# Ten of span 0's twelve attention pairs alone, the last two beside the first three products of L1, and weight blocks stored in one run

## The chip, the cores and the metric

The kernel runs on one core of a Trainium2 chip. The metric is the device time of one launch in microseconds, the median of several runs; one further execution was recorded by the profiler. PE is TensorE, DVE is VectorE, ACT is ScalarE, POOL is GpSimd, and SP is the engine whose queue issues most DMAs.

## The reference

An attention with normalised queries and keys is followed by a two-layer feed-forward network. There are 8 batches, 12 heads, 448 positions and a head size of 64; the network is 768 to 2048 to 768. All is float32 in the reference, and the weights come as 64-bit floats.

```python
def rmsnorm(x, g):
    rms = np.sqrt(np.mean(x * x, axis=-1, keepdims=True) + 1e-06)
    return x / rms * g
q_n, k_n = (rmsnorm(q, g_q), rmsnorm(k, g_k))
scores = scale * np.matmul(q_n, k_n.transpose(0, 1, 3, 2))
attn = np.exp(scores - np.max(scores, axis=-1, keepdims=True))
attn = attn / (np.sum(attn, axis=-1, keepdims=True) + 1e-09)
attn_out = np.matmul(attn, v)
...
x = attn_out.transpose(0, 2, 1, 3).reshape(B * S, H * D)
h = x @ w_in
r = np.maximum(h, 0.0)
return (r * r) @ w_out
```

## The kernel before

Two batches make a span, so there are four spans of 896 tokens. A *pair* is two heads of one batch; a span has twelve pairs. A pair's output is one 128-row part of xT, the network's input with the channels on partitions: `xT[:, b, hp]` for batch b of the span and pair hp of the batch.

The two layers are computed with a seven-product scheme (Winograd's form of Strassen's) on 2x2 blocks: the two batches are the two column blocks, and channels are halved on both sides. `A11, S2, S1, S3, A12, A22, S4` name the seven combinations of weight blocks, and T1 to T4 with B11, B21, B22 those of the input. T1 to T4 are made by `combine_x` in xC and in part of xT as pairs come out. For the first layer (L1) there are HF = 8 column blocks f, each with seven products; a product is three matmuls over 448 columns, which the trace shows as six, into one PSUM bank. Its results are added up by DVE (z, y, and the sums g22, g21, g12) and squared after a relu. The product of A22 accumulates in the bank pd on top of S3, and S4 in pc on top of S1, after DVE has read the first one. A product takes a *block* of weights, `sw`, which SP loads from DRAM (`w1s`, `w2s`) five products ahead (`load_blocks`). The second layer (L2) does the same with gT and gC.

There are two forms of attention. Pairs with i < NAT (the twelve of span 0) are done *alone* by `attention_alone`: keys in four chunks of 112, sums by a matmul with ones (`total_of`), transposes by PE, the square root on ACT and DVE (`roots`). The others are done in the *later* form by `attention`, whose steps are interleaved with L2's products of the span before: four 64x64 matmuls side by side on PE, sums by DVE's `add_up` and `fold`, then sent out and spread again by two DMAs that POOL issues (`sums["out"]`, `spread`), a norm with a power on POOL (`norm_by_squares`), transposes by DVE. Then `finish` scales the values with the sums.

The weights are turned from 64-bit floats into float32 and into the seven combinations during span 0, in small steps called ticks: `prepare(t)` has four ticks for each of 32 pieces of weights (t is the piece that enters). A piece takes a load of 768 KB, two activations on ACT (L589, L606), three operations on DVE (L603, L608, L613), the add of the low words (L575 on POOL for the first pieces, L579 on DVE for the others), and on average two sums on POOL (L583). Every second piece ends in a store of 1344 KB by SP. `weights(upto)` runs the ticks up to a number; `EARLY` (52) is the number done in the alone stage and `ALL` (140) the end.

The schedule is written by hand: each engine executes its instructions in the order of the Python code, which the generators' `yield` interleave. Blocks that have not been stored can't be loaded, so the ticks come ahead of the products that need them.

Of the kernel before, what the change touches and what calls it, by code (L numbers as in the profile page):

```python
# [10 lines left out]
F32 = mybir.dt.float32  # L11
# [376 lines left out]
def attention_then_ffn_bounded(  # L388
# [53 lines left out]

    NAT = 2 * NPAIR

# [43 lines left out]

    EARLY, ALL = 4 * 13, 4 * (2 * NFC + 3)
    assert DM == NW and BLOCKS * 8 * HW + EXPS * NW + 2 * NW <= 3 * HF * S and 2 * NW <= 4 * S and HF % 4 == 0  # L490
# [4 lines left out]
    A21 = 7  # L495
    w1s = dram.tile([HF, 7, P, HW], F32, name="w1s")
    w2s = dram.tile([7, HF // 4, P, 4, HW], F32, name="w2s")

# [52 lines left out]
    def prepare(t):  # L551
# [10 lines left out]
        def value(n, half):  # L562
            if not there(n):
                return

            to = ((A11, A12), (A21, A22)) if n < NFC else ((A11, A21), (A12, A22))
            places = [place_of(n, k) for k in to[n % 2]]
            part = slice(half * HW, (half + 1) * HW)
            if not doubles:
                nc.gpsimd.tensor_copy(blocks_of(n)[:, places[half]], words_of(n).bitcast(F32)[:, part])  # L570
                return
            _, eu, low, _ = parts(n)
            if n < EARLY // 4:
                dst = blocks_of(n)[:, places[half]]
                nc.gpsimd.tensor_tensor(*[x.bitcast(I32) for x in (dst, low[:, part], eu[:, part])], ALU.add)  # L575
            elif half == 0:
                dst = blocks_of(n)[:, places[0]:places[1] + 1:places[1] - places[0]]
                low, eu = (x.rearrange("p (h m) -> p h m", h=2) for x in (low, eu))
                nc.vector.tensor_tensor(*[x.bitcast(I32) for x in (dst, low, eu)], ALU.add)  # L579
# [14 lines left out]
        if there(n) and n % 2:  # L594
            c = n % NFC // 2
            dst = w1s[c] if n < NFC else w2s[:, c // 4, :, c % 4]
            first = place_of(n, A11)
            nc.sync.dma_start(dst.rearrange("k p m -> p k m"), blocks_of(n)[:, first:first + 7])
            written[0] = n + 1
# [43 lines left out]
    uses2 += [(m, i) for m in range(HC) for i in (S2, S1, S3, A22, S4)]  # L643
    def order_of(span, f):

        return (A11, A12, S2, S1, S3, A22, S4) if span == f == 0 else range(7)

# [3 lines left out]
    def load_blocks(upto):  # L651

        while len(stream) < min(upto, NSPAN * (N1 + N2)):
            n = len(stream) % (N1 + N2)
            if written[0] < min(2 * (n // 7 + 1) if n < N1 else 2 * NFC, 2 * NFC):
                return
            sw = loads.tile([P, 4, P], F32, tag="sw", name="sw", bufs=5)
            if n < N1:
                sw = sw[:, 0:HC]
                src = w1s[n // 7, order_of(len(stream) // (N1 + N2), n // 7)[n % 7]].rearrange("p (c m) -> p c m", c=HC)  # L660
            else:
                n -= N1
                m, i = uses2[n // (HF // 4)]
                src = w2s[i, n % (HF // 4), :, :, m * P:(m + 1) * P]
            nc.sync.dma_start(sw, src)
            stream.append(sw)
# [250 lines left out]
    def attention_alone():  # L917


        for i in range(NAT):  # L920
# [22 lines left out]
            if i + 2 < NAT:  # L943
                norm(i + 2)
            elif not more:
                norm(NAT)
                load(NAT + 2)
# [3 lines left out]
            load_v(i + 1)  # L951
            if i + 2 < NAT:
                roots(i + 2)
            yield
            scores(i, 2)
            scores(i, 3)
            total_of(i - 1)
            values(i, (0, 1))
# [5 lines left out]
            if NAT <= i + 3 < NAT + 2:  # L964
                load(i + 3)
            yield
        values(i, (2, 3))
        total_of(i)
        finish(i)
        combine_x(i)  # L970

    def attention(first):


        last = first + 2 * NPAIR
        for i in range(first, last + 1):
# [56 lines left out]

    def first_product(work, span):

# [3 lines left out]
        def activate(g, src):  # L1039
# [3 lines left out]
            else:  # L1043
                nc.gpsimd.tensor_tensor(g, g, g, ALU.mult)  # L1044

        for f in range(HF):
            n = span * (N1 + N2) + f * 7
            order = order_of(span, f)
            g11, g12 = gT[:, f, 0:S], gT[:, f, S:2 * S]
# [3 lines left out]
            for at, i in enumerate(order):  # L1053
# [4 lines left out]
                if first and into == "pa":  # L1058
                    if span == 0 and f:
                        ps_of[into] = ps_o.tile([P, S], F32, tag="ot"[f % 2], name="pa")  # L1060
                    else:
                        ps_of[into] = ps_s.tile([P, 2, 512], F32, tag="s", name="pa")[:, 0, 0:S]
                elif first:
                    ps_of[into] = bank(into)
# [5 lines left out]
                if i == A11:  # L1070
                    p1 = work.tile([P, S], F32, tag="p1", name="p1", bufs=1)
                    nc.scalar.copy(p1, ps)  # L1072
                elif i == S2:
                    z = work.tile([P, S], F32, tag="z", name="z")
                    add(z, p1, ps, ALU.add)  # L1075
                elif i == S1:
                    y = work.tile([P, S], F32, tag="y", name="y")
                    add(y, z, ps, ALU.add)
                elif i == A12:
                    activate(g11, ps)  # L1080
                else:
                    g, x = {S3: (g22, y), A22: (g21, z), S4: (g12, z)}[i]
                    add(g, x, ps, ALU.add)  # L1083
                    activate(g, g)
# [91 lines left out]
    with tc.tile_pool(name="words", bufs=2) as spare["pool"]:  # L1176
# [5 lines left out]
        with tc.tile_pool(name="first", bufs=2, reuse_waits="tile") as work:  # L1182
# [9 lines left out]
            for u, _ in enumerate(attention_alone()):  # L1192

                weights(min(EARLY, 4 + (EARLY - 4) * u // (4 * NAT - 7)))
                if u == 4 * NAT - 9:
                    load_blocks(5)
        with tc.tile_pool(name="first_product", bufs=2, reuse_waits="tile") as work:
            for u, _ in enumerate(first_product(work, 0)):
                if u == 6:

                    left = ps_s.tile([P, 2, 512], F32, tag="s", name="bits")
                    banks["bits"] = left.rearrange("p a b -> p (a b)")[:, 0:NW].bitcast(U32)
                weights(min(ALL, EARLY + (ALL - EARLY) * (u - 1) // (N1 - 6)))
                if u == N1 - 5:
                    norm(NAT + 1)
                if u == N1 - 4:
                    transposes(NAT)
                    squares(NAT + 2)
    for span in range(NSPAN):
# [7 lines left out]
        with tc.tile_pool(name="second_product", bufs=2, reuse_waits="tile") as work:  # L1217
            rest = second_product(work, span)
            if more:
# [4 lines left out]
                total, done, most = HC * (7 * HF + 4) - 20, 0, 10 * NPAIR + 1  # L1224
                for u, _ in enumerate(attention(nxt)):
                    while done < total * min(u + 1, most) // most + 3 * max(u + 1 - most, 0):
                        next(rest)
                        done += 1
# [90 lines left out]
```

## Time and profile before

| | us |
|---|---|
| median of 3 runs (lowest, highest) | 1363.51 (1362.49, 1364.83) |
| the profiled execution's own time | 1362.31 |
| its span | 1360.5 |
| start of the alone stage's second pair to the end of pair 9 | 15.5 to 111.6 |
| pairs 10 and 11 alone | 111.6 to 133.9 |
| L1 of span 0 | 133.9 to 264.9 |
| from L2 of span 0 to the end | 264.9 to 1360.5 |

The span is what the profiler saw from the first to the last instruction; the launch's time has 1.8 us more. A line such as `L1083` is the line of the kernel's file that issued the instruction. "Idle before" is time in which an engine had nothing to do ahead of an instruction, with the instruction or DMA that ended it. A matmul's length overlaps with its neighbours', so PE's rate is read from the distance of starts.

### The profile page before, as it was taken

To read this page: it belongs to the slowest core of one execution; us is meant where nothing else is said; L and a number is where in the kernel's file an instruction comes from. 1 tells how busy PE (TensorE), PEld (TensorE's weight loads), DVE (VectorE), ACT (ScalarE), POOL (GpSimd) and SP (SyncE) were. 2 spreads that over 40 slices of the span, in tenths; PEclk is the share of its full clock that TensorE was granted. 3 is DMA by queue.
4 is the path that set the end of the run, shared out by engine and by line. 5 is a ranking of instruction groups with operands and counts; after the bars stand their busy time and mean duration, and the time that the engine had idled before them with its cause. 6 is when DMAs were issued, how large, how long until landed. Compare 5 with 4: busy or idle time off the path is not lost.

```text
span 1360.5 us, 16880 instructions
## 1 busy us (share of the span) xinstructions
PE 1340.5 (99%) x5618; PEld 641.6 (47%) x5618; DVE 832.1 (61%) x1482; ACT 430.0 (32%) x674; POOL 566.0 (42%) x458
## 2 busy tenths in 40 slices
PE   8999999999999999999999999999999999999998
PEld 3333445444444455444444455444444455555554
DVE  6999788599987333467778523557788633332111
ACT  7886466433332011233332111233333211110000
POOL 5667533466563122655565222446566312220000
PEclk9999999999999999999999999999999999999999
DMA  9777999655685333355675433345765443334443
GB/s 240 208 229 198 314 360 327 183 130 111 130 151 129 99 87 88 100 119 118 135 150 115 113 100 87 101 104 118 142 129 110 105 103 87 87 91 107 106 111 71
DMA packets 434084, 190.12 MB, mean 140 GB/s; under 512 B 282948, under 2 KB 430788, under 8 KB 433988
## 3 DMA queue, kind: packets, MB, share of 16 engines
q1 hardware_dynamic: 427364, 180.33, 52.2%
q0 software_dynamic: 4736, 8.40, 2.5%
q8 instruction: 47, 0.77, 0.2%
q10 hardware_dynamic: 1888, 0.23, 0.1%
q14 instruction: 49, 0.40, 0.1%
HBM read 155.72 MB, written 33.16 MB: 139 GB/s over the span
## 4 chain that ended last, share of the span: by engine, by line
PE 90%; DVE 5%; ACT 3%; DMA 1%; issue 1%; SPq 0%; POOL 0%; ACTq 0%; DVEq 0%
PE ps L1134 37%; PE pd L1068 10%; PE pa L1068 10%; PE pc L1068 10%; PE sc L785 7%; PE pav L862 7%; PE pb L1068 5%; ACT gT L797 1%; DVE gT L810 1%; DVE rstd L715 1%; PE sc L793 1%; DVE gC L613 1%; PE tot L876 1%; DMA gT<-in_moe_w_in_dram 1%; PE pav L851 1%
## 5 line engine op out<-in xcount | busy, mean ns | idle before, releaser
L1134 PE MATMUL ps<-gT,sw 128*128 128x448 f32 x752 | 293.0, 543 | 0.0
L1134 PE MATMUL ps<-gC,sw 128*128 128x448 f32 x576 | 225.2, 543 | 0.0
L1044 POOL TENSOR_TENSOR gT<-gT 128x448 f32<-128x448 f32 x96 | 93.9, 980 | 283.3 <-ACT gT L1040 283.3
L1134 PEld LDWEIGHTS ps<-gT,sw 128*128 128x128 f32 x752 | 141.1, 190 | 146.4 <-issue 142.0
L750 POOL TENSOR_TENSOR half<-half,mhalf 128x28 f32<-128x28 f32 x36 | 175.2, 4868 | 72.7 <-DVE half L749 69.2
L1134 PEld LDWEIGHTS ps<-gC,sw 128*128 128x128 f32 x576 | 108.1, 190 | 112.9 <-issue 110.7
L1068 PE MATMUL pa<-xT,sw 128*128 128x448 f32 x384 | 155.0, 540 | 0.6 <-ACT p L1072 0.6
L1040 ACT ACTIVATE gT<-gT 128x448 f32<-128x448 f32 x96 | 55.3, 577 | 311.2 <-DVE gT L1083 311.2
L787 ACT ACTIVATE pr<-sc 128x896 f32<-128x896 f32 x87 | 77.5, 915 | 121.7 <-PE sc L785 121.7
L785 PE MATMUL sc<-qkT 64*64 64x448 f32 (+1 forms) x1152 | 109.8, 496 | 0.0
L1068 PEld LDWEIGHTS pa<-xT,sw 128*128 128x128 f32 x384 | 72.9, 190 | 72.6 <-issue 70.7
L583 POOL TENSOR_TENSOR gC<-gC 128x384 f32<-128x384 f32 x64 | 76.2, 1209 | 62.2 <-DVE gC L579 60.4
L1083 DVE TENSOR_TENSOR gT<-z,pd 128x448 f32<-128x448 f32 x32 | 19.8, 620 | 97.8 <-PE pd L1068 97.6
L1068 PE MATMUL pd<-xT,sw 128*128 128x448 f32 x192 | 77.9, 542 | 1.3 <-DVE z L1075 1.3
L1068 PE MATMUL pd<-xC,sw 128*128 128x448 f32 x192 | 77.5, 540 | 1.3 <-DVE gT L1083 1.3
L1068 PE MATMUL pb<-xC,sw 128*128 128x448 f32 x192 | 77.5, 540 | 0.1
L752 POOL TENSOR_TENSOR qk<-qk,half 128x448 f32<-128x448 f32 x72 | 76.4, 1081 | 2.8
L1068 PE MATMUL pc<-xC,sw 128*128 128x448 f32 x192 | 77.4, 539 | 0.0
L1068 PE MATMUL pc<-xT,sw 128*128 128x448 f32 x192 | 77.4, 539 | 0.0
L830 POOL DMA_DIRECT2D xT<-factors x72 | 38.0, 532 | 94.7 <-DMA factors<-square 63.9
L862 PE MATMUL pav<-pr,vt 64*64 64x448 f32 x348 | 72.7, 537 | 0.0
L862 PE MATMUL rest<-pr,vt 64*64 64x448 f32 x348 | 72.7, 537 | 0.0
(144 smaller groups left out, 1849.6 us busy)
## 6 DMA issues: line engine op xcount, KB each, us to landing
sw<-w1s SPq DMA_DIRECT2D x224, 192.0 KB, 2.4
sw<-w2s SPq DMA_DIRECT2D x168, 256.0 KB, 3.2
w1s<-gC SPq DMA_DIRECT2D x8, 1344.0 KB, 6.4
w2s<-gC SPq DMA_DIRECT2D x8, 1344.0 KB, 6.1
out_dram<-osb SPq DMA_DIRECT2D x186, 56.0 KB, 1.9
qk<-in_q_dram SPq DMA_DIRECT2D x144, 56.0 KB, 3.5
qk<-in_k_dram SPq DMA_DIRECT2D x144, 56.0 KB, 3.0
xT<-factors POOLq DMA_DIRECT2D x72, 112.0 KB, 3.4
```

The lines of the kernel that those rows point to most:

```text
L583: nc.gpsimd.tensor_tensor(*[blocks_of(n)[:, place_of(n, i)] for i in (dst, x, y)], op)
L750: nc.gpsimd.tensor_tensor(half, half, mhalf, ALU.pow)
L752: nc.gpsimd.tensor_tensor(qkn[:, s], raw[:, s], half[:, s * NG:(s + 1) * NG].rearrange("p g -> p g ()").to_broadcast([P, NG, 32]), ALU.mult)
L785: nc.tensor.matmul(sc[part, h, 0:n], qkT[rows, 0, 1, keys], qkT[rows, 0, 0, of], start=True, stop=True)
L787: nc.scalar.activation(pr, sc[:, :, 0:n], AF.Exp)
L830: nc.gpsimd.dma_start(xT[h * D:(h + 1) * D, b % 2, hp], sums["out"][i % 2].rearrange("(h g) t -> h () (g t)", h=2)[h].to_broadcast([D, S]))
L862: nc.tensor.matmul(into, vs[i][rows, h, c, :], probs[i, c][rows, h, :], start=(c == 0), stop=(c == NF), skip_group_check=True)
L1040: nc.scalar.activation(g, src, AF.Relu)
L1044: nc.gpsimd.tensor_tensor(g, g, g, ALU.mult)
L1068: nc.tensor.matmul(ps, stream[n + at][:, c], rhs[:, c], start=first and c == 0, stop=c == HC - 1, skip_group_check=not first)
L1083: add(g, x, ps, ALU.add)
L1134: nc.tensor.matmul(ps, stream[n][:, c % 4], rhs_of[i][:, c], start=c == 0, stop=c == HF - 1)
```

## The change

NAT becomes ten: pairs 10 and 11 of span 0 are done in the later form. Beside them L1 begins: `first_product(work, 0, 0)` does the three products A11, S1 and A12 of six of the eight column blocks (NE = 6), which need no result of those two pairs. A11's and S1's results are kept in gT by a copy on ACT; A12 accumulates on A11 and is squared. When both pairs are through, the second call does S2, S3, A22 and S4 of those six blocks, and all seven of the last two. For the kept blocks DVE makes y from z and the kept S1, one operation with both inputs in SBUF, and S4 has a bank of its own.

The ticks are spread anew: 48 by the end of the alone stage, 86 by the end of the two pairs, 140 before the end of L1. POOL keeps the add of the low words for 21 pieces instead of 13. `roots` stands behind the last two scores of a pair. Blocks of all seven combinations lie side by side in `w1s` and `w2s`, so a store writes 10,752 bytes in one run per partition instead of seven runs of 1536.

```diff
@@ -440,7 +440,8 @@
     sides = [slice(m * P // 2, (m + 1) * P // 2) for m in range(2)]
-    NAT = 2 * NPAIR
+    NAT = 2 * NPAIR - 2
+    NE = HF - 2
     def start_of(span):
         return 2 * span * NPAIR
@@ -486,15 +487,15 @@
     HW = HC * P
     WORDS, BLOCKS, EXPS = 7, 2, 4
-    EARLY, ALL = 4 * 13, 4 * (2 * NFC + 3)
+    EARLY, MID, ALL = 48, 86, 4 * (2 * NFC + 3)
     assert DM == NW and BLOCKS * 8 * HW + EXPS * NW + 2 * NW <= 3 * HF * S and 2 * NW <= 4 * S and HF % 4 == 0
     A11, S2, S1, S3, A12, A22, S4 = range(7)
     A21 = 7
-    w1s = dram.tile([HF, 7, P, HW], F32, name="w1s")
-    w2s = dram.tile([7, HF // 4, P, 4, HW], F32, name="w2s")
+    w1s = dram.tile([HF, P, 7, HW], F32, name="w1s")
+    w2s = dram.tile([HF // 4, P, 4, 7, HW], F32, name="w2s")
     def pairs_of(words):
         both = words.rearrange("p (n two) -> p n two", two=2)
@@ -570,7 +571,7 @@
                 nc.gpsimd.tensor_copy(blocks_of(n)[:, places[half]], words_of(n).bitcast(F32)[:, part])
                 return
             _, eu, low, _ = parts(n)
-            if n < EARLY // 4:
+            if n < MID // 4:
                 dst = blocks_of(n)[:, places[half]]
                 nc.gpsimd.tensor_tensor(*[x.bitcast(I32) for x in (dst, low[:, part], eu[:, part])], ALU.add)
             elif half == 0:
@@ -593,9 +594,9 @@
         n = t - 3
         if there(n) and n % 2:
             c = n % NFC // 2
-            dst = w1s[c] if n < NFC else w2s[:, c // 4, :, c % 4]
+            dst = w1s[c] if n < NFC else w2s[c // 4, :, c % 4]
             first = place_of(n, A11)
-            nc.sync.dma_start(dst.rearrange("k p m -> p k m"), blocks_of(n)[:, first:first + 7])
+            nc.sync.dma_start(dst, blocks_of(n)[:, first:first + 7])
             written[0] = n + 1
         if there(t) and doubles:
             e, eu, low, high = parts(t)
@@ -641,9 +642,9 @@
     uses2 = [(m, i) for m in range(HC) for i in (A11, A12)]
     uses2 += [(m, i) for m in range(HC) for i in (S2, S1, S3, A22, S4)]
-    def order_of(span, f):
-        return (A11, A12, S2, S1, S3, A22, S4) if span == f == 0 else range(7)
+    first_uses = [(f, i) for f in range(NE) for i in (A11, S1, A12)]
+    first_uses += [(f, i) for f in range(NE) for i in (S2, S3, A22, S4)]
+    first_uses += [(f, i) for f in range(NE, HF) for i in range(7)]
     N1 = HF * 7
     N2 = HC * 7 * (HF // 4)
@@ -651,17 +652,19 @@
     def load_blocks(upto):
         while len(stream) < min(upto, NSPAN * (N1 + N2)):
-            n = len(stream) % (N1 + N2)
-            if written[0] < min(2 * (n // 7 + 1) if n < N1 else 2 * NFC, 2 * NFC):
+            span, n = divmod(len(stream), N1 + N2)
+            if n < N1:
+                f, i = divmod(n, 7) if span else first_uses[n]
+            if written[0] < (2 * (f + 1) if n < N1 and span == 0 else 2 * NFC):
                 return
             sw = loads.tile([P, 4, P], F32, tag="sw", name="sw", bufs=5)
             if n < N1:
                 sw = sw[:, 0:HC]
-                src = w1s[n // 7, order_of(len(stream) // (N1 + N2), n // 7)[n % 7]].rearrange("p (c m) -> p c m", c=HC)
+                src = w1s[f, :, i].rearrange("p (c m) -> p c m", c=HC)
             else:
                 n -= N1
                 m, i = uses2[n // (HF // 4)]
-                src = w2s[i, n % (HF // 4), :, :, m * P:(m + 1) * P]
+                src = w2s[n % (HF // 4), :, :, i, m * P:(m + 1) * P]
             nc.sync.dma_start(sw, src)
             stream.append(sw)
@@ -943,17 +946,16 @@
             if i + 2 < NAT:
                 norm(i + 2)
             elif not more:
-                norm(NAT)
                 load(NAT + 2)
             yield
             if more:
                 transpose(i + 1, 0, 0)
             load_v(i + 1)
-            if i + 2 < NAT:
-                roots(i + 2)
             yield
             scores(i, 2)
             scores(i, 3)
+            if i + 2 < NAT:
+                roots(i + 2)
             total_of(i - 1)
             values(i, (0, 1))
             finish(i - 1)
@@ -963,16 +965,20 @@
             combine_x(i - 1)
             if NAT <= i + 3 < NAT + 2:
                 load(i + 3)
+            if i + 2 >= NAT:
+                norm(i + 2)
             yield
+        transposes(NAT)
         values(i, (2, 3))
         total_of(i)
         finish(i)
         combine_x(i)
-    def attention(first):
-        last = first + 2 * NPAIR
+        if NAT + 2 < 2 * NPAIR:
+            squares(NAT + 2)
+    def attention(first, last):
         for i in range(first, last + 1):
             if i < last:
                 scores(i, 0)
@@ -1031,7 +1037,7 @@
             sub(gC[:, 2, f], g21, gC[:, 1, f], ALU.subtract)
             sub(g12, g22, g12, ALU.subtract)
-    def first_product(work, span):
+    def first_product(work, span, part=1):
         B11, B21, B22 = xT[:, 0, 0:HC], xT[:, 0, HC:], xT[:, 1, HC:]
         T1, T2, T4, T3 = xC[:, 0], xC[:, 1], xC[:, 2], xT[:, 1, 0:HC]
@@ -1043,9 +1049,29 @@
             else:
                 nc.gpsimd.tensor_tensor(g, g, g, ALU.mult)
+        if part == 0:
+            for f in range(NE):
+                turn[0] += 1
+                pa, pc = bank("pa"), bank("pc")
+                for at, (ps, rhs) in enumerate(((pa, B11), (pc, T1), (pa, B21))):
+                    n = 3 * f + at
+                    load_blocks(n + 5)
+                    for c in range(HC):
+                        nc.tensor.matmul(ps, stream[n][:, c], rhs[:, c], start=at < 2 and c == 0,
+                                         stop=c == HC - 1, skip_group_check=at == 2)
+                    if at < 2:
+                        nc.scalar.copy(gT[:, HF + f, at * S:(at + 1) * S], ps)
+                    else:
+                        activate(gT[:, f, 0:S], ps)
+                    yield
+            return
         for f in range(HF):
+            kept = span == 0 and f < NE
+            order = (S2, S3, A22, S4) if kept else range(7)
             n = span * (N1 + N2) + f * 7
-            order = order_of(span, f)
+            if span == 0:
+                n = 3 * NE + 4 * f if kept else 7 * f
             g11, g12 = gT[:, f, 0:S], gT[:, f, S:2 * S]
             g21, g22 = gT[:, HF + f, 0:S], gT[:, HF + f, S:2 * S]
             add = nc.vector.tensor_tensor
@@ -1056,7 +1082,7 @@
                              A12: ("pa", B21), A22: ("pd", T4), S4: ("pc", B22)}[i]
                 first = into not in ps_of
                 if first and into == "pa":
-                    if span == 0 and f:
+                    if span == 0:
                         ps_of[into] = ps_o.tile([P, S], F32, tag="ot"[f % 2], name="pa")
                     else:
                         ps_of[into] = ps_s.tile([P, 2, 512], F32, tag="s", name="pa")[:, 0, 0:S]
@@ -1072,14 +1098,17 @@
                     nc.scalar.copy(p1, ps)
                 elif i == S2:
                     z = work.tile([P, S], F32, tag="z", name="z")
-                    add(z, p1, ps, ALU.add)
+                    add(z, g21 if kept else p1, ps, ALU.add)
+                    if kept:
+                        y = work.tile([P, S], F32, tag="y", name="y")
+                        add(y, z, g22, ALU.add)
                 elif i == S1:
                     y = work.tile([P, S], F32, tag="y", name="y")
                     add(y, z, ps, ALU.add)
                 elif i == A12:
                     activate(g11, ps)
                 else:
-                    g, x = {S3: (g22, y), A22: (g21, z), S4: (g12, z)}[i]
+                    g, x = {S3: (g22, y), A22: (g21, z), S4: (g12, y if kept else z)}[i]
                     add(g, x, ps, ALU.add)
                     activate(g, g)
                 if span and f and i in (S1, A22):
@@ -1194,18 +1223,26 @@
                 weights(min(EARLY, 4 + (EARLY - 4) * u // (4 * NAT - 7)))
                 if u == 4 * NAT - 9:
                     load_blocks(5)
+        with tc.tile_pool(name="early_product", bufs=2, reuse_waits="tile") as work:
+            places_for(work, 1)
+            places.append(qkT[:, 1])
+            places.extend(gT[:, n:n + 2, S:2 * S] for n in range(0, NE, 2))
+            halves[:] = [xC[:, n, HC - 1].rearrange("p (h q) -> p h q", h=2) for n in (1, 2)]
+            sums_for(work)
+            rest, done, ticks_here = first_product(work, 0, 0), 0, 5 * (2 * NPAIR - NAT) + 6
+            for u, _ in enumerate(attention(NAT, 2 * NPAIR)):
+                weights(EARLY + (MID - EARLY) * (u + 1) // ticks_here)
+                while done < 3 * NE * (u + 1) // ticks_here:
+                    next(rest)
+                    done += 1
+            for _ in rest:
+                pass
         with tc.tile_pool(name="first_product", bufs=2, reuse_waits="tile") as work:
+            left = ps_s.tile([P, 2, 512], F32, tag="s", name="bits")
+            banks["bits"] = left.rearrange("p a b -> p (a b)")[:, 0:NW].bitcast(U32)
             for u, _ in enumerate(first_product(work, 0)):
-                if u == 6:
-                    left = ps_s.tile([P, 2, 512], F32, tag="s", name="bits")
-                    banks["bits"] = left.rearrange("p a b -> p (a b)")[:, 0:NW].bitcast(U32)
-                weights(min(ALL, EARLY + (ALL - EARLY) * (u - 1) // (N1 - 6)))
-                if u == N1 - 5:
-                    norm(NAT + 1)
-                if u == N1 - 4:
-                    transposes(NAT)
-                    squares(NAT + 2)
+                weights(min(ALL, MID + (ALL - MID) * (u + 1) // (N1 - 3 * NE - 4)))
+                ahead(u + 3 * NE, start_of(1))
     for span in range(NSPAN):
         more = span + 1 < NSPAN
         nxt = start_of(span + 1)
@@ -1222,7 +1259,7 @@
                 halves[:] = [work.tile([P, 2, S // 2], F32, tag=f"half{m}", name="half", bufs=1) for m in range(2)]
                 sums_for(work)
                 total, done, most = HC * (7 * HF + 4) - 20, 0, 10 * NPAIR + 1
-                for u, _ in enumerate(attention(nxt)):
+                for u, _ in enumerate(attention(nxt, nxt + 2 * NPAIR)):
                     while done < total * min(u + 1, most) // most + 3 * max(u + 1 - most, 0):
                         next(rest)
                         done += 1
```

## The prediction

> **What bounds the kernel now.** I read the page first. Its busy line and PE slices say that PE is nearly never idle, but "busy" includes a matmul that is held back, so I go on to stages.
>
> ```profile
> PE 1340.5 (99%) x5618; PEld 641.6 (47%) x5618; DVE 832.1 (61%) x1482; ACT 430.0 (32%) x674; POOL 566.0 (42%) x458
> ...
> PE   8999999999999999999999999999999999999998
> ```
>
> Next, busy time by stage, cut at PE's own events: pairs 2 to 9 of span 0 alone, pairs 10 and 11 alone, L1, then attention beside L2. Columns: stretch, its length, busy us (instructions) of each engine, clock, DMA share, GB/s.
>
> ```profile
> 29.40:111.60 82.20, 78.29 (x403) 29.65 (x401) 78.23 (x114) 66.82 (x122) 51.46 (x40) 1.00 0.76 220
> 111.60:133.90 22.30, 22.01 (x115) 8.15 (x113) 21.65 (x34) 14.40 (x24) 16.67 (x10) 1.00 0.83 209
> 133.90:264.90 131.00, 127.57 (x342) 63.48 (x340) 98.89 (x133) 70.76 (x110) 59.55 (x54) 1.00 0.87 301
> 264.90:459.40 194.50, 194.50 (x1106) 91.13 (x1106) 164.24 (x315) 61.44 (x85) 101.71 (x77) 1.00 0.62 127
> ```
>
> In the alone stage DVE has 78.2 of 82.2 us and PE the same: two bounds, 10.27 us a pair. From 264.9 us on PE is full, and the change touches nothing there, so its worth is what it does to the instant at which attention of span 1 begins, now 264.86. PE's timeline gives the pieces (start, length, instructions, [idle before <- releaser]).
>
> ```profile
> 90.52 1.76 PE L793 MATMUL sc<-qkT 64*112 64x448 f32 x8
> ...
> 111.60 1.76 PE L793 MATMUL sc<-qkT 64*112 64x448 f32 x8
> ...
> 133.89 2.52 PE L1068 MATMUL pa<-xT,sw 128*128 128x448 f32 x6
> ...
> 143.90 2.42 PE L1068 MATMUL pd<-xT,sw 128*128 128x448 f32 x6
> 147.63 2.52 PE L1068 MATMUL pd<-xC,sw 128*128 128x448 f32 x6 [1.31 <-DVE gT L1083]
> 149.99 2.42 PE L1068 MATMUL pc<-xT,sw 128*128 128x448 f32 x6
> ```
>
> Pairs 8 and 9 took 111.60 - 90.52 = 21.08 us. Products follow each other every 2.256 us, so 56 need 126.3 of L1's 131.0: 4.6 are waits. One is S3 then A22: both accumulate in pd, and A22 may not start before DVE (L1083) has read S3. Starts 3.73 apart instead of 2.256: 1.47 lost.
>
> **What the Trainium skill says.** "PSUM — Partial Sum Buffer", The four PSUM rules: a matmul without the first-flag adds to what the element holds, so a partial sum has to be read before the next product lands on it; the 1.31 above is that wait. "SBUF — State Buffer", Who interferes with whom: a DVE instruction with two SBUF inputs contends with a GpSimd instruction that reads SBUF. The trace fits: L810, the 896-wide add, averages 1.74 us in the alone stage, beside the weights' POOL adds, and 1.05 beside L2; L583 on POOL averages 1.41 there and 1.07 in L1. "DMA: Bandwidth & Descriptors", Why small descriptors are slow: some 3 cycles a packet beside 32 bytes a cycle. For the old 1536-byte runs that is 3 in 51, an estimate of 0.4 us of a store's 6.4. No run here shows it yet.
>
> **The change, part by part.**
>
> Removed: two middle pairs alone (the last pairs keep their lighter form): -21.1 us. Added on PE: two pairs in the later form. At 279.49 to 284.92 one such pair takes 2.8 for scores and 2.6 for values: +10.9 for two. The products stay 56. L1's old waits go, since its f=0 order goes: -4.6. Sum so far **-14.8 us**. That is the most that PE alone could give.
>
> Pace of the alone stage: 44 ticks of weights over 33 steps instead of 48 over 41, so 5.33 a pair, not 4.68. A tick costs DVE 2.84 / 4 = 0.71 us there (L603 0.73, L608 1.13, L613 0.98), so 0.46 a pair, 3.2 over seven pairs if DVE is the limit. Against it, the roots now stand behind the last two scores, so the exps no longer queue behind ACT's wait for DVE (L725 <- L716: 14.0 us in 8 waits). PE's floor in a pair is some 9.65, so at most 0.6 a pair comes back. Bounds -2 and +3.5; I take **+1.4**, since DVE has only 5% free.
>
> Entry of the beside stage: scores(10) need DVE's transposes of pair 10, queued behind finish(8), combine_x(8) and norm(11) of the last step. In the trace the finish in that place ends at 132.65 and PE is through at 133.9. Then come 0.62 for one subtraction, 2.2 for the norm's reduce and small ops, 1.2 for the transposes, 0.67 for ACT's gain: 137.3, a wait of 3.4; norm(12)'s DVE work is no longer ahead of that finish, which gives some back. Bounds 1 and 4; **+2.9**.
>
> Beside stage: PE has 18 x 2.256 + 10.9 = 51.5 us. Twelve extra copies and squares on ACT cost PE nothing while S1 stands between A11 and A12; ACT has about 40 us of work in 51. I put **+0.5** (0 to 3). POOL is the doubtful one: 38 ticks x 1.3 us (32 adds in 41.9 us in the alone stage) = 49.4, and attention besides. SP's stores wait for those adds, and block loads stand behind them; five blocks ahead, or 14 us, cover it.
>
> Its tail is what S2 waits for. In POOL's order from the start of scores(10): norm(11)'s pow and two multiplies end at 5.2; 23 ticks until the second pair's sums, 29.9; first pair's two DMA issues and the wait between, 4.5; combine_x(10) there, three at 1.13, 3.4. That is 43.0. Then sums out (0.6 + 2.8) and spread (0.5 + 3.4) make 50.3. On DVE: finish 1.3, three ticks 2.1, combine 1.9, so 55.6; five ticks 4.0; z and y 1.2; one tick 0.95; g22 0.61: 62.4. PE would start f=0's A22 at 51.5 + 4.5 = 56.0. So S2 and A22 together wait 6.4. Nothing hides it: PE has no other work in order. Bounds 2 (uncontended adds) and 12 (POOL at 1.5 a tick, DVE late too); **+6.4**.
>
> Rest of L1: kept blocks run S2, S3, A22, S4, so the S3-A22 adjacency that the trace shows once comes six times. DVE has z, y and about 1.6 ticks to do during S3's 2.256 us. An undelayed add costs 0.85 (drain 0.15, hand-over 0.1, add 0.61); with a 1.9 us tick in the way up to 2.7. For the five that the tail does not hold already I take the measured 1.47: **+7.3** (4 to 12). DVE's extra add per block lies in this same chain. f=6 and 7 keep the old order.
>
> Behind A22's wait stand S4 and the next block on PE, and ACT's relu of the sums; behind the entry's wait the first product, whose five blocks are loaded by then.
>
> Loads: pairs 10 and 11 now take eight DMAs for q and k and four for v on SP instead of three and one, at about 0.33 us of SP each, 5 us in all. load(12), issued in pair 9, has to wait there until POOL has read raw pair 10; load(13), at the first step of the beside stage, until it has read pair 11, 5.2 us in, and v of pair 11 and the sixth block queue behind. The sixth block is due at 1.7 + 5 x 2.9 = 16, so I put 0 (bounds 0 and 2).
>
> At nothing: stores and loads in the new layout (loads are five ahead; a store's 0.4 us is behind POOL anyway, and longer strides between read pieces are under the same cover); POOL keeping the value adds to n=21 (POOL idles 51 of 75 us in the middle of L1); norm(12), moved from pair 11 into L1 beside norm(13), with its 0.95 on ACT, 2.2 on DVE and 7.1 on POOL (the same slack, and stores of w2 are not read until L2). If that cover were gone, late w2 blocks would hold L2's first product.
>
> Sum: -14.8 + 1.4 + 2.9 + 0.5 + 6.4 + 7.3 = **+3.7 us**. The profiled execution is 1362.31 (span 1360.5 and 1.8 around it): 1366.0. The median of the runs is 1.2 above it, so 1367.2.
>
> **Rivals.**
>
> Faster: DVE and POOL keep up. For it: POOL idles in waits each alone pair, DVE is in L2's stage at 84% without holding PE, and uncontended adds are a third shorter. Then pace -2, entry 2, tail and f=0 1.5, five adjacencies at 0.85, 4.3: -14.8 + 5.8 = -9.0, or 1354.5. Against it: DVE's sum in the beside stage is about 48 of 51 us, in order, with waits on ACT and POOL.
>
> Slower still, by the other mechanism: POOL sets the stage. Its sum over the whole stage is 5.2 + 49.4 + 9.0 + 3.4 = 67 against 51.5. If its lag passes the five loaded blocks, a store that waits for L583 holds SP and the blocks behind it, and ACT's next exponents wait for their slot. The stage then takes POOL's time, +15.5 instead of 6.4 and 0.5: +12.3, or 1375.8. It decides from a lag of about 14 us. Against it: the lag grows late in the stage and L1 gives POOL slack.
>
> Not doing what it says: stores may still go out in 1536-byte packets although each partition's run is seven times as long. The page's packet counts would then stay as they are. As the layout is priced at nothing, the time stays 1367.2.
>
> **How the numbers follow.** Measurements of this kernel tell about 0.2%, 2.7 us. Forecast case 0.55, itself +0 to +8 (1363 to 1371): slower 0.33, same 0.20, faster 0.02. Faster case 0.25: faster 0.21, same 0.04. POOL case 0.20: slower 0.19, same 0.01. Together faster 0.23, same 0.25, slower 0.52. The range reaches into both rivals: 1357 to 1377.
>
> **What would show it.** The first pa of L1 near 113 us, after an idle of 2 to 3.5 before pair 10's scores; alone pairs at 10.3 to 10.7; second S2 phase about 51 us after those scores, with waits on DVE's combine or g22; five further waits of 0.8 to 2.5 us at pd <- DVE g22; attention of span 1 at about 268.5 instead of 264.86, and everything after it as before. Wrong, if PE's waits in 113 to 265 sum below 10 us, if POOL holds SP so that PE waits for sw, or if later stages move.

## The result, and the profile after

The kernel after takes **1406.32 us** (median of 4 runs, 1403.64 to 1407.91) against 1363.0 for the kernel before (four runs): ratio 1.0315, 95% interval 1.0294 to 1.0336. That is 43 us slower, where 4 were forecast and 13.5 was the upper end. The profiled execution took 1403.64.

The page of the kernel after, its busy line and the PE slices:

```profile
PE 1344.4 (96%) x5646; PEld 641.7 (46%) x5646; DVE 851.8 (61%) x1494; ACT 431.4 (31%) x668; POOL 608.1 (43%) x488
...
PE   8997868899999999999999999999999999999998
```

A slice is 35 us. PE has slices of 7, 8, 6, 8 and 8 from 105 us on, where the kernel before has nines. By stage (kernel after; the columns are those of the prediction): the last two pairs alone, the stage beside the pairs up to the first S2, the rest of L1, everything later.

```profile
92.36:115.40 23.04, 22.25 (x114) 8.05 (x112) 22.40 (x36) 15.24 (x25) 18.73 (x11) 1.00 0.67 178
122.68:197.20 74.52, 57.14 (x236) 25.63 (x237) 60.13 (x66) 36.23 (x54) 57.82 (x48) 0.91 0.74 251
197.20:305.40 108.20, 93.39 (x228) 44.66 (x228) 67.89 (x99) 48.87 (x76) 44.59 (x37) 0.95 0.67 224
305.40:1401.80 1096.40, 1089.44 (x4673) 531.18 (x4672) 614.47 (x1168) 256.13 (x382) 420.40 (x335) 1.00 0.48 110
```

The last stage took 1095.6 before and 1096.4 now, so all is lost before attention of span 1 begins: at 305.40 instead of 264.86, +40.5. Against the sums that PE alone would need:

| stage | needed by PE | took | loss | forecast |
|---|---|---|---|---|
| alone, ten pairs (end) | 112.8 | 115.4 | 2.6 | 1.4 |
| wait before pair 10's scores | 0 | 7.3 | 7.3 | 2.9 |
| beside the pairs | 51.5 | 74.5 | 23.0 | 0.5 + 6.4 |
| rest of L1 | 85.7 | 108.2 | 22.5 | 7.3 |

-14.8 + 55.4 = +40.6: the table closes. What PE waited for (kernel after; total us, times, longest):

```profile
PE pb L1094 <- DMA sw<-w1s: 10.9, 2, 7.6
PE pd L1094 <- DVE gT L1112: 10.4, 6, 2.9
PE sc L788 <- ACT qkT L765: 7.2, 1, 7.2
...
PE pa L1060 <- DMA sw<-w1s: 6.1, 1, 6.1
PE pc L1060 <- ACT gT L1046: 2.2, 1, 2.2
```

The largest is a load of a block, 17 us in three waits. SP's queue in the same trace shows why the load is late (first its waits, then two stretches of its instructions):

```profile
SPq L599 <- POOL gC L584: 41.9, 8, 8.9
```

```profile
148.53 1.26 SPq L706 DMA_DIRECT2D vt<-in_v_dram  x2
159.48 0.34 SPq L599 DMA_DIRECT2D w1s<-gC  x1
159.92 1.34 SPq L668 DMA_DIRECT2D sw<-w1s  x2
...
274.80 1.37 SPq L668 DMA_DIRECT2D sw<-w1s  x3
283.75 0.32 SPq L599 DMA_DIRECT2D w2s<-gC  x1
```

```profile
153.70 5.75 POOL L584 TENSOR_TENSOR gC<-gC 128x384 f32<-128x384 f32 x4
```

From 149.8 to 159.5 SP stands before one store, whose sums POOL ends at 159.4. The blocks behind it belong to column blocks that had been stored long before. PE runs dry at 159.8 and goes on at 165.95. The block that it then gets could have been asked for at about 150.7, when the product that used its buffer was done. SP asked for it at 159.92, and it was there at 165.95; PE had four products left to run meanwhile, 9.2 us. The second stretch, 276 to 283.7, is held by the sums behind norm(13)'s power.

One cost has no wait of its own. Below are stretches of the kernel after, right behind waits of 7.2, 6.1, 7.6, 2.4, 2.85 and 3.3 us. After the busy times of the five engines stands the granted clock of PE, as a share of the full one:

```profile
122.68:125.95 3.27, 3.27 (x17) 0.87 (x17) 3.10 (x6) 0.92 (x1) 3.27 (x1) 0.50 0.97 285
...
165.95:170.60 4.65, 4.65 (x10) 1.85 (x10) 4.58 (x4) 0.00 (x0) 4.57 (x5) 0.52 0.95 385
...
197.21:201.60 4.39, 4.39 (x7) 2.16 (x8) 2.20 (x2) 0.00 (x0) 4.31 (x5) 0.56 0.70 274
...
238.15:242.30 4.15, 4.15 (x7) 2.06 (x8) 1.68 (x2) 1.93 (x3) 2.31 (x3) 0.59 0.59 235
...
263.63:266.10 2.47, 2.47 (x7) 1.36 (x8) 0.00 (x0) 1.94 (x3) 2.39 (x4) 1.00 0.00 0
290.18:294.10 3.92, 3.92 (x7) 1.93 (x8) 0.00 (x0) 0.00 (x0) 0.00 (x0) 0.61 1.07 428
```

After five of these six waits PE runs at about half its clock for some 4 us: the first scores take 3.27 us instead of 1.67, and from a product to the next start it is 3.9 to 4.6 instead of 2.256. The five places cost 1.6 + 2.4 + 2.0 + 1.8 + 1.6 = 9.4 us, which the table has in its losses. The Trainium skill, "TensorE: Matmul & The Clock Gate", Part 1, What's actually happening, has the clock halved after at least one idle window of about 3.4 us, and these windows run freely, whatever the kernel does. The traces agree in part. In the kernel after and in its twelve variants below, every wait of PE of 3.44 us or more was followed by the half clock. Among shorter waits it is mixed: the shortest with it took 1.97 us and the longest without it 3.36, both in e1_order, and the 2.85 us that went without it here had it in e7_values_dve:

```profile
255.22 3.99 PE L1094 MATMUL pd<-xC,sw 128*128 128x448 f32 x6 [2.85 <-DVE gT L1112]
```

So a wait shorter than that window can be enough, which the page does not say.

### The profile page after: what moved, and what is told of

Same layout as the page of the kernel before. It is cut to its first block, busy times and chain, and to the rows that moved or that the text cites. A ratio compares the mean times of both kernels' runs of the same rounds, so it can differ in the third digit from the quotient of the medians.

```text
span 1401.8 us, 17013 instructions
## 1 busy us (share of the span) xinstructions
PE 1344.4 (96%) x5646; PEld 641.7 (46%) x5646; DVE 851.8 (61%) x1494; ACT 431.4 (31%) x668; POOL 608.1 (43%) x488
## 2 busy tenths in 40 slices
DMA packets 428836, 190.66 MB, mean 136 GB/s; under 512 B 290756, under 2 KB 423428, under 8 KB 426692
## 4 chain that ended last, share of the span: by engine, by line
PE 82%; DVE 9%; POOL 3%; DMA 3%; issue 2%; ACT 1%; SPq 0%; POOLq 0%; DVEq 0%; ACTq 0%
PE ps L1163 36%; PE pd L1094 9%; PE pc L1094 9%; PE pa L1094 8%; PE sc L788 7%; PE pav L865 7%; PE pb L1094 4%; DVE gC L614 1%; POOL gC L584 1%; DVE gT L813 1%; DMA sw<-w1s 1%; DMA factors<-square 1%; DVE gC L604 1%; PE sc L796 1%; DVE gC L580 1%
## 5 line engine op out<-in xcount | busy, mean ns | idle before, releaser
L753 POOL TENSOR_TENSOR half<-half,mhalf 128x28 f32<-128x28 f32 x38 | 184.2, 4848 | 94.5 <-DVE half L752 88.0
L1163 PEld LDWEIGHTS ps<-gC,sw 128*128 128x128 f32 x576 | 108.2, 190 | 112.8 <-issue 109.5
L1094 PE MATMUL pa<-xT,sw 128*128 128x448 f32 x312 | 125.8, 540 | 0.0
L788 PE MATMUL sc<-qkT 64*64 64x448 f32 (+1 forms) x1216 | 117.5, 502 | 7.2 <-ACT qkT L765 7.2
L1094 PE MATMUL pb<-xC,sw 128*128 128x448 f32 x192 | 81.1, 561 | 11.9 <-DMA sw<-w1s 10.9
L1094 PE MATMUL pd<-xC,sw 128*128 128x448 f32 x192 | 79.7, 552 | 10.4 <-DVE gT L1112 10.4
L1094 PEld LDWEIGHTS pa<-xT,sw 128*128 128x128 f32 x312 | 59.4, 190 | 57.8 <-issue 57.3
L755 POOL TENSOR_TENSOR qk<-qk,half 128x448 f32<-128x448 f32 x76 | 80.8, 1083 | 3.0
L788 PEld LDWEIGHTS sc<-qkT 64*64 64x64 f32 x1216 | 42.7, 134 | 57.3 <-issue 40.3
```

The source lines that it names most:

```text
L753: nc.gpsimd.tensor_tensor(half, half, mhalf, ALU.pow)
L755: nc.gpsimd.tensor_tensor(qkn[:, s], raw[:, s], half[:, s * NG:(s + 1) * NG].rearrange("p g -> p g ()").to_broadcast([P, NG, 32]), ALU.mult)
L788: nc.tensor.matmul(sc[part, h, 0:n], qkT[rows, 0, 1, keys], qkT[rows, 0, 0, of], start=True, stop=True)
L1094: nc.tensor.matmul(ps, stream[n + at][:, c], rhs[:, c], start=first and c == 0, stop=c == HC - 1, skip_group_check=not first)
L1163: nc.tensor.matmul(ps, stream[n][:, c % 4], rhs_of[i][:, c], start=c == 0, stop=c == HF - 1)
```

## The experiments

My theory after the result: POOL's queue is too long beside the pairs, SP stands before its stores, and PE starves; behind that, the work on the weights has lost its cover. Rivals: slow DMA (the layout), the order of the products, the pairs' own chain.

**e1_order**, S4 ahead of A22 in the kept blocks.

```diff
-            order = (S2, S3, A22, S4) if kept else range(7)
+            order = (S2, S3, S4, A22) if kept else range(7)
```

> The kernel after, with the kept blocks in the order S2, S3, S4, A22, so that S4 stands between S3 and the product that accumulates on it. Theory (the adjacency makes PE wait for DVE): the six waits at pd, 11.3 us by distances of starts (1.4, 1.5, 1.6, 2.6, 1.3, 3.0), go; since DVE has a product more for each sum, L1's second part gets 8 to 11 us shorter and the kernel comes to 1395 to 1398. Rival (DVE is saturated there, 1.6 ticks a product, and the wait only moves to the next bank): under 3 us.

1407.24 us (ratio to before 1.0328, 1.0311 to 1.0346): nothing gained. The wait had moved, as the rival said:

```profile
PE pb L1094 <- DMA sw<-w1s: 11.3, 2, 7.9
PE pb L1094 <- DVE gT L1112: 11.1, 5, 4.2
```

Three results of a block in two banks in turn put the next block's S2 on A22's bank.

**e5_banks**, the same order with pd in a third bank.

```diff
+                elif first and into == "pd" and kept:
+                    ps_of[into] = ps_o.tile([P, S], F32, tag="ot"[f % 2], name="pd")
```

> The kernel after, with the kept blocks in the order S2, S3, S4, A22 as in e1_order, and pd of the kept blocks in one of the two banks that A11 and A12 use elsewhere, in turn. e1_order only moved the wait: with three of a block's results in two banks in turn, the next block's S2 came to land on A22's bank. Theory (the wait is PE's, for a bank that DVE has not read, and DVE has the time on average): waits of PE for DVE in the second part fall from 11 us to under 3, time 8 to 11 us below the kernel after, 1395 to 1398. Rival (DVE is saturated in the second part: 54 ticks at 3.42 us for four, 46 us, and 40 adds at 0.62, 25 us, in 86 us, with waits on ACT): the waits move again, to another bank, and the gain is under 4 us.

1400.19 us (1.0278, 1.0254 to 1.0301), 6 below after, though the two intervals overlap a little. PE's wait for DVE is 6.3 in three places, down from 10.4 in six, between theory and rival: the adjacency was real, but DVE is late there by itself.

**e2_store_pool**, POOL issues the stores.

```diff
-            nc.sync.dma_start(dst, blocks_of(n)[:, first:first + 7])
+            nc.gpsimd.dma_start(dst, blocks_of(n)[:, first:first + 7])
```

> The kernel after, with the stores of the weight blocks issued by POOL's queue instead of SP's. POOL makes the sums that a store waits for, so the store has nothing to wait for there, and SP's queue has no store in it. Theory (head of the line: POOL is late with the sums, SP stands before a store, the loads of blocks that were stored long ago stand behind it, and PE waits for sw): PE's waits for sw, 17 us listed and some 20 by starts, go to under 3; POOL pays about 1 us for each of 11 stores; kernel 12 to 18 us faster, 1388 to 1394. Rival (DMA itself is slow: blocks take 5.1 us to land instead of 2.4): PE waits for sw stay above 12 us, time within 5 us.

1393.32 us (1.0225, 1.0208 to 1.0242), 13 below after. PE's waits:

```profile
PE pd L1094 <- DVE gT L1112: 12.9, 6, 3.8
PE pc L1060 <- ACT gT L1046: 7.5, 1, 7.5
PE sc L788 <- ACT qkT L765: 7.2, 1, 7.2
PE pb L1094 <- DMA sw<-w1s: 1.8, 1, 1.8
```

The head of the line is shown: 17 us of waits for blocks became 2.5. POOL's lateness then came through by another way, ACT. In the kernel after ACT's L590 had waited 4.8 us for POOL's L576.

**e3_norm_late.** In this kernel pair 14's squares are taken before its load, so only its time is used.

```diff
-        if u == 7 * (HF - 2):
+        if u == 7 * (HF - 2) + (10 if nxt == start_of(1) else 0):
             norm(nxt + 1)
```

> The kernel after, with norm(13) and load(14) ten products later in L1 of span 0, behind the last tick of the weights. Theory (the power of norm(13), 4.8 us on POOL and 2.1 of multiplies, holds the last sums, these the store, and SP the blocks: PE waits 5.1 us at S2 of the last column block): that wait goes, 4 to 5 us faster, 1401 to 1402. Rival (sums are late by themselves): no change within 1.5 us, the wait stays.

1398.16 us (1.0260, 1.0243 to 1.0277), 8 below after; by the traces attention of span 1 begins at 302.5 instead of 305.4. The wait of 3.3 us at the last S2, with the half clock behind it, is gone from the trace, as the theory had it. The edit moves the load of pair 14 too, eight DMAs that held SP from 268.8 to 274.7 us in the kernel after, so it doesn't part the norm from the load. The theory had 4 to 5 us, the traces give 2.9 and the runs 8; I can't place the difference.

**e4_old_layout**, w1s and w2s as before.

> The kernel after, with w1s and w2s laid out as before, seven runs of 1536 bytes per partition in a store. Theory (the layout is off PE's path): within 2 us of the kernel after, 1404 to 1408; blocks land as late as in it. Rival (long runs occupy the DMA engines, so that small DMAs land late: sums out took 4.6 and 6.6 us instead of 2.8, blocks 5.1 instead of 2.4): 10 to 20 us faster, and those times back at 2.8 and 2.4.

1406.97 us (1.0329, 1.0311 to 1.0346): the layout is worth nothing that shows, and PE waits for blocks as in after (19 us). The rival is out. Nor were blocks slow: from the first scores of pair 10 on they landed in 4.8 us in after, and in 4.9 in L1 of the kernel before (medians; the 2.4 in the text above is that of the whole run). The pages also settle the prediction's last rival: this kernel has 441,124 DMA packets and after 428,836, and the 12,288 between them are 16 stores of 128 partitions with seven packets or one. Stores landed in 7.4 and 6.1 us here (w1s and w2s, medians) and in 7.2 and 5.8 in after, near the 0.4 us that the prediction had estimated, and off PE's path.

**e6_mid66**, fewer ticks beside the pairs. In this kernel a result overwrites the low words of weight piece 30 before they are used.

```diff
-    EARLY, MID, ALL = 48, 86, 4 * (2 * NFC + 3)
+    EARLY, MID, ALL = 48, 66, 4 * (2 * NFC + 3)
...
-            if n < MID // 4:
+            if n < 21:
```

> The kernel after, with 66 instead of 86 ticks done by the end of the two pairs (18 beside them instead of 38, 74 in the second part instead of 54); POOL keeps the value adds of 21 pieces as before. Theory (POOL's queue is what is too long beside the pairs): the stage from scores(10) to the first S2, 74.5 us now, comes down to 52 to 57, with no wait for sw in it; the second part, 108 us now, grows, since DVE has 63 us of ticks and 25 of adds in 86: 112 to 118. Sum 8 to 16 us faster, 1390 to 1398. Rival (the pairs' own chain of sums, two DMAs and finish sets the stage): it stays above 65 us, and the kernel is slower than after.

1398.63 us (1.0263, 1.0241 to 1.0285), 8 below after. The two stages, and what PE waited for:

```profile
123.95:179.69 55.74, 55.11 (x236) 25.46 (x237) 39.84 (x52) 27.75 (x44) 35.91 (x32) 0.95 0.76 233
179.69:302.12 122.43, 98.79 (x228) 46.63 (x228) 82.07 (x112) 57.29 (x87) 64.21 (x53) 0.90 0.71 245
```

```profile
PE pd L1094 <- DVE gT L1112: 17.1, 6, 4.2
```

With 18 ticks instead of 38 the stage beside the pairs is 55.7 us instead of 74.5, so the pairs' own chain does not set it. But the 20 ticks cost 14.2 of these 18.8 us in the next stage, through DVE: PE's waits for DVE there are 19.4 us instead of 11.4, and half clocks come to 10.8 us instead of 5.4 (by starts against 2.256).

**e7_values_dve**, nine pieces' adds on DVE.

```diff
-            if n < MID // 4:
+            if n < EARLY // 4:
```

> The kernel after, with the add of the low words of pieces 12 to 20 on DVE instead of POOL (18 adds of about 1.2 us less on POOL, nine of 0.95 more on DVE), ticks at their places. Theory (POOL is the bound beside the pairs, with DVE next): the stage from scores(10) to the first S2 comes from 74.5 to 62 to 67 us, waits for sw fall to under 5; the second part as it was; kernel 1394 to 1399. Rival (DVE is the bound there): no gain, 1404 to 1410.

1396.58 us (1.0243, 1.0224 to 1.0261), 10 below after; the stage beside the pairs is 63.5 us (124.96 to 188.46). Theory right there, though PE still waited 10.3 for blocks, 3.3 of it and the half clock at the place that e3 cured.

**e8_before_roots**, the kernel before with its roots moved.

> The kernel before, with the roots of a pair behind the last two scores as in the kernel after, nothing else. Theory (DVE has 95% of the alone stage, so ACT's order gives little): within 2.7 us of the kernel before. Rival (ACT's wait of 1.75 us a pair for DVE stood ahead of the exps, and PE waited for these): alone stage 0.4 to 0.6 us a pair shorter, 4 to 6 us faster, 1357 to 1359.

1363.63 us over 12 runs (1.0008, 1.0000 to 1.0017): worth nothing.

**e9_before_no_w2 and e10_after_no_w2**, arithmetic of the second layer's weights left out.

```diff
-        if there(t) and doubles:
+        if there(t) and doubles and t < NFC:
```

and so in `value`, `total` and `unsigned`.

> The kernel before, with the arithmetic on the second layer's weights left out (pieces 16 to 31: no operation of theirs on ACT, DVE or POOL; their loads and stores stay, so L2 uses other numbers). It is the control for e10_after_no_w2. Theory: PE's waits in L1, 4.6 us, mostly go, nothing else: 1358 to 1361. Rival (the weights hold the kernel before too): below 1355.

> The kernel after, with the same arithmetic on the second layer's weights left out as in e9_before_no_w2. Theory (what costs is the weights' work, which had 22 us of alone stage and 131 of L1 as cover and has lost about 11 us of PE's time there, while DVE and POOL were nearly full): waits for sw go, six waits at pd of 0.8 to 0.9 stay, the entry's 7.2 stays; -14.8 + 2.6 + 7.2 + 5.1 + 1: 1362 to 1367, within 8 us of e9_before_no_w2. Rival (the new structure itself costs: the pairs' chain, the entry, the banks): 20 us or more above e9_before_no_w2.

1361.94 us (0.9993, 0.9985 to 1.0001) and 1378.56 us (1.0106, 1.0083 to 1.0129). This pair is the main finding. The same work costs **1 us in the kernel before and 28 in the kernel after** (1406.3 - 1378.6), of the 43 that were lost. ACT, DVE and POOL lose their part of it together, so the pair doesn't tell which engine's part costs. PE's waits in e10:

```profile
PE sc L788 <- ACT qkT L765: 7.2, 1, 7.2
PE pa L1060 <- DMA sw<-w1s: 6.1, 2, 4.9
PE pd L1094 <- DVE gT L1112: 4.3, 6, 0.7
```

With DVE free of the second layer's ticks the adjacency is six equal waits of 0.71. The remaining 16.6 between the two kernels is more than the 8 of my theory and less than the rival's 20: the entry, the adjacency, and still waits for blocks, since the first layer's ticks remain beside the pairs, with SP before their stores.

**e11_combined**: stores by POOL, e5's order and bank, and the transposes of pair 10 ahead of norm(11).

```diff
-            if i + 2 >= NAT:
+            if i + 2 >= NAT and more:
                 norm(i + 2)
             yield
         transposes(NAT)
+        norm(NAT + 1)
```

> The kernel after with three cures together: stores issued by POOL as in e2_store_pool, order and banks of e5_banks, and the transposes of pair 10 ahead of norm(11) on DVE at the end of the alone stage. The last is new: in the trace of after DVE's four small copies of norm(11) took 3.6 us instead of 0.8 while POOL was busy, and the transposes of pair 10, whose input POOL had finished at 117.3, began at 121.3 behind them. Theory: the entry's wait falls from 7.2 to 3.5 to 4.5 us, and gains add up: -13 - 6 - 3: 1383 to 1387. Rival (all of them lean on one engine that is full, DVE, so that what one gives the next takes): 1388 to 1395. Neither expects less than before's 1363.

1386.84 us (1.0166, 1.0144 to 1.0188), in the theory's range by the total, but not for its reason. The entry's wait fell from 7.2 to 2.6, and yet from the end of the last sums to the first S2 it took 73.8 us (118.1 to 191.85) where e2 took 74.3 (117.0 to 191.28). What PE gained at the start it waited for later: 4.1 us for a block and 4.8 for ACT, both with the half clock behind them, where e2 had 7.5 for ACT. ACT goes on in both kernels when POOL has added the low words, at nearly the same time (e2, then e11):

```profile
181.67 0.90 ACT L590 ACTIVATE gC<-words 128x768 f32<-128x768 f32 x1 [10.76 <-POOL gC L576]
182.32 0.89 ACT L590 ACTIVATE gC<-words 128x768 f32<-128x768 f32 x1 [7.32 <-POOL gC L576]
```

So POOL's queue sets that stage in these two kernels, and the earlier start of PE is not in series with it.

**e12_combined_dve**, POOL's adds end at piece 16.

> e11_combined with the add of the low words on DVE from piece 16 on instead of 21 (POOL 10 adds less, DVE five more). In e2_store_pool PE still waited 7.5 us for ACT, which waited for POOL's adds beside the pairs. Theory (POOL is still the longer of the two there): that wait goes, 3 to 7 us below e11_combined. Rival (DVE is now the longer): within 2 us of it or slower.

1390.46 us (1.0192, 1.0170 to 1.0214), slower than e11: the wait of 4.8 us for ACT went and one for DVE came, so DVE is then the longer.

```profile
PE pb L1097 <- DVE xC L916: 7.2, 1, 7.2
```

**e13_two_first and e14_combined_two_first**, two products ahead of pair 10's scores.

```diff
+            for _ in range(2):
+                next(rest)
+                done += 1
             for u, _ in enumerate(attention(NAT, 2 * NPAIR)):
```

> The kernel after, with the first two products (A11 and S1 of f=0, whose operands and blocks are there) ahead of the scores of pair 10, in the 7.2 us that PE waits at the entry. Theory (POOL's queue sets the end of the stage beside the pairs, so what PE gains at its start it waits for later; only the half clock of 3.3 us after the wait goes): the entry's wait falls to about 3 us and the first scores take 1.7 instead of 3.3, but the first S2 comes no more than 2 us earlier and the kernel is within 2 us of after, 1402 to 1407. Rival (the losses of the stages add up): 4.5 + 1.6 us are gained, 1398 to 1401.

> e11_combined with the first two products ahead of the scores of pair 10. There SP no longer stands before stores, and the entry's wait is 2.6 us. Theory: the wait goes whole, and with it the half clock behind it (1.6 us); of the 4.2 us POOL's lag, which ACT passes on (4.8 us at 183.7 in e11_combined), takes back 2 to 4: 1383 to 1386. Rival (the losses add up): 1381 to 1383.

1405.94 us (1.0312, 1.0288 to 1.0336) and 1386.73 us (1.0180, 1.0159 to 1.0200): no gain, but both miss their purpose. The second product waited in the place of the scores:

```profile
PE pc L1060 <- issue: 7.1, 1, 7.1
```

By the code its bank is the one that holds pair 9's values until `finish(9)`; the start fits, but no run isolates it. Little of the idle time was filled, so these two don't tell whether the losses add up; e11 against e2 shows that at the entry they do not. No version comes near the kernel before, and none of these runs points to one.

## Why the prediction was wrong

**The side was right.** The kernel is slower, the later stages did not move (+0.8), and layout (e4) and roots (e8) are worth nothing. That PE's own work fell by 14.8 us stays a sum; no run reaches it.

**The step that failed: the cover of the block loads, and with it which case was likely.** The forecast rested on "five blocks ahead, or 14 us, cover it". The rival with POOL's queue, at 0.20, is what happened, with SP before a store and ACT's exponents waiting for their slot, as it named them. I had compared POOL's lag with 14 us of products, but the cover is shorter. A load can be asked for only when its buffer is free, so four products stand before the one that needs it, 9.2 us where the products follow each other, and the landing comes out of these as well. SP, which waits in program order for each store by itself, stood for 9.7 us before one, the block took 6.0 to land, and PE waited 6.1. The sum for the tail put pair 11's sums at 43.0 us after the first scores; they were issued at 51.5, and their DMA took 6.6 instead of 2.8. S2 then waited for its block, not for the tail: DVE's combine ended at 193.9, the block was there at 197.2.

**The rival's own price, +15.5, was too low** against 23.0. It has POOL's 67 us less PE's 51.5. By the trace POOL was busy for 57.8 us, DMA issues among them, so its adds were not dearer than priced. But it also stood for 15.3 us in its queue, before the pairs' DMAs and DVE's share of their sums (kernel after, 122.68 to 197.2):

```profile
POOL xT L833 <- DMA factors<-square: 11.3, 2, 6.7
POOL factors L1022 <- DVE square L827: 4.0, 1, 4.0
```

The sum has 9.0 for these waits and the issues together. Why the DMA took so long is not shown. The price has no half clock either, which is 1.6 + 2.4 us of PE's time in this stage.

**Rest of L1, 7.3 against 22.5.** The adjacency, starts against 2.256, cost 1.4, 1.5, 1.6, 2.6, 1.3 and 3.0: 11.3 for six, or 1.9 each instead of the 1.47 measured once. The larger missing parts are terms that I had put at nothing. The norm in its new place holds the last sums and by them SP: 5.1 with its half clock (e3 removes it, with the load moved too). Half clocks elsewhere: 3.8. Another bank wait: 1.1. The remaining 1.2 is in small steps.

**Entry, 2.9 against 7.3.** I had DVE's small operations at their price alone. In the trace the four copies took 3.57 instead of 0.78, beside POOL's multiplies and adds (kernel after, DVE):

```profile
116.62 3.57 DVE L750 COPY other<-half 32x28 f32<-32x28 f32 x4
120.22 0.94 DVE L751 TENSOR_TENSOR half<-half,other 128x28 f32<-128x28 f32 x1
```

And norm(10), which I took for a relief, stood where norm(12) had stood, so finish(8) ended at 114.9 and not at 111.6. e11 cut the wait but not the stage: beside a full POOL it was not in series.

**The sum that I did not make** is that of each engine over the whole window, from 29.4 us to the start of attention of span 1 (kernel before, then after; busy us of PE, PEld, DVE, ACT, POOL):

```profile
29.40:264.90 235.50, 227.88 (x854) 101.28 (x852) 198.76 (x278) 151.99 (x255) 127.68 (x102) 1.00 0.83 264
29.40:305.40 276.00, 230.61 (x867) 100.30 (x865) 219.21 (x288) 152.67 (x248) 171.16 (x134) 0.94 0.72 226
```

DVE was busy for 84% before. With 15 us less and the same work it would have had to reach 90%, more than the 75% that it had managed in L1, though less than the 95% of the alone stage. And the work did not stay the same: DVE's busy time rose by 20 us and POOL's by 43. How much of this is added work and how much slower instructions is not parted. I priced stage by stage, each with slack borrowed from the next. e6 shows that ticks moved out of one stage are paid in the other, and e9 with e10 that the second layer's part of this work is 27 of the 43 us. That the sum would have decided the case beforehand is argued, not shown.

## What to carry to other kernels

When a stage is shortened under work that it hides, add up the hidden work over the whole window that remains, engine by engine, before pricing any edit: a saving on the bounding engine can be lost whole once the work under it is the longer, as here. In an in-order queue a store that waits for a late engine delays every load behind it, however early those could go; the queue of the engine that makes its data is the better place, here by 13 us. And price a wait of 2 us or more on TensorE with the slow clock that may follow it, some 2 us in these traces.

## What the hardware showed that I had not expected

TensorE's clock halved after waits as short as 1.97 us (e1_order), for about 4 us, some 2 us of loss each; it always did from 3.44 us up, and one of 3.36 us went without.

Copies of 28 elements, 0.2 us each, took 0.9 each while POOL worked without a break, and the add of 28 elements behind them 0.94 instead of 0.19. The add has two inputs in SBUF, so it fits the contention that the prediction quotes; the copies have one, so for them that sentence is not enough, and no run isolates the cause.
